# Attention head and token mixer on one core: half-height stores with 8 KB rows, plain relus, narrower pp and another instruction order

## The chip, the cores and the metric

The kernel runs on 1 core of one Trainium2 chip. The metric is device time in microseconds (us). The kernel before takes 110.91 us, the median of 3 runs (110.85 to 111.06).

## What is computed

There are 8 batches of 8 heads, 576 tokens and 64 columns a head. A small set of 32 queries p attends to k and v and packs them; the tokens' queries q then attend to the packed rows. The result, with the heads side by side (576 x 512), goes through a token mixer:

```
p_packed = softmax(p k^T / 8) v
x        = softmax(q p_packed^T / 8) p_packed        # then 576 x 512 per batch
wq, wk   = x w_q, x w_k                              # 512 -> 64 each
W_tok    = (wq wk^T) / 8                             # 576 x 576
out      = relu(W_tok x) w_out                       # 512 -> 512
```

All inputs and the output are float32 in memory; matmuls are made in bfloat16.

## The kernel before

The whole program is one list of steps, ORDER, written out in full and run through from left to right: each item is a step name, a batch and part, an engine (@V is VectorE, DVE; @A ScalarE, ACT; @P GpSimd, POOL) and after "=" the PSUM banks that it takes. PE's steps name no engine. Each engine runs its own steps in the order of the list, and waits for what the others must have done first. DMA issues are steps too: LD steps of q, k, v and w_out (wout) are issued by POOL, because they cast float32 to bfloat16 on the way; K0 and K1 (batch 0's k) and all ST and STF steps (stores) are issued by SyncE (SP); p and w_q, w_k are issued by ACT. An issue stands in its engine's queue like any other instruction.

The steps of a batch b, with their lines:

- LD.k, LD.q, LD.v (L181, L185, L177): 576 KB each at the destination. k and q take one transfer over 128 partitions, v two over 64 partitions each. Four buffers of each kind.
- SET.v (L206): a memset that puts columns of ones at both ends of a v buffer, on DVE.
- KT (L249): 32x32 block transposes of k on DVE. S1 (L261): p times k on PE. X1 (L266): exp on ACT. TE (L270): blocks transposed back on DVE. PV (L282): times v and the ones columns, on PE. RC (L287) and PP (L294): the reciprocal of the row sums, and pp, the packed rows normalised and masked. PT: pp transposed, both on DVE.
- QV: q transposed on DVE in three pieces. S2 (L339): q times the packed rows, on PE. X2 (L344): exp. RS (L354), RR (L359): row sums and reciprocals on DVE. AM (L365): normalised rows, on POOL or DVE, in two or three pieces. AT (L374): transposed on PE. AE: evicted from PSUM.
- QK (L306) and QKE: pp times w_k and w_q. WKQ (L396, L401) and WE: wk and wq. GM (L422), GE, Y (L432), YE: the mixer regrouped so that 576 x 576 is never formed. MX (L446) and MR (L452): W_tok x for 512 and for 64 tokens. RL, RLF, RLR (L457 on ACT, L459 on DVE): relu.
- OT (L491): times w_out, 16 matmuls of 128x512 a batch and 4 for the remaining tokens of two batches. OE, OEF: evicted to SBUF as float32. ST (L511 for the remaining tokens, else L496), STF (L496): stored.

The steps of neighbouring batches are interleaved, so that PE works on the OT of batch b while the attention of b+1 and b+2 runs. WARM steps are matmuls on a zero tile that keep PE busy where it would wait (57 of them). The relu (turn, L464) also puts the tokens into another order on the way, so that in a store each partition holds two neighbouring tokens: a store covers 128 partitions (64 groups times two halves) with 4 KB rows, two of four token tiles at a time. The output has 10 half buffers of 128x1024. A store's place in SP's queue sets when it can go: ST.3.4 is the second in the queue and waits for the remaining tokens of batches 2 and 3.

```
    def turn(eng, o, i):
        relu(eng, o.rearrange("a (t g y) -> a t y g", g=GR, y=2), i.rearrange("a (t y g) -> a t y g", g=GR, y=2))
...
        dst = out[b].rearrange("(g r) n -> g r n", r=R)[:, 0:8].rearrange("g (y t) n -> g y (t n)", y=2)
        nc.sync.dma_start(dst[:, :, t * D:t * D + n], o)
```

Of the kernel before, what the change touches and what calls it, by code (L numbers as in the profile page):

```python
# [7 lines left out]
NL, NB, NO, NE = 4, 3, 10, 2  # L8

ORDER = """  # L10
SET.warm LD.P0 LD.P1 LD.P2 LD.P3 LD.W0 LD.W1 LD.K0 LD.k1 LD.K1 SET.mask@V KC.0@V SET.v0@V LD.v0 PC@V
LD.q0 KT.0.0@V KC.1@A SET.v3@V PX@V KT.0.1@V SET.v1@V WARM.27=0 S1.0=0,1,2,3 SET.idf@V KT.1.2@V
SET.aff@P X1.0.1@A LD.k2 WC.0@P SET.aT0@V TE.0.1@V WARM.4=4 S1.1=4,5,6,7 LD.v1 SET.v2@V X1.1.1@A
X1.0.0@A LD.q1 X1.1.0@A TE.0.0@V LD.v2 SET.aT1@V TE.1.1@V WARM.6=2 PV.0.0=2,3 LD.k4 PV.0.1 QV.0.1@V
WC.1@P QV.0.0@V LD.q2 RC.0.1@V RC.0.0@V PP.0.1@V QV.0.2@V PP.0.0@V PT.0@V LD.k3 KT.2.2@V WARM.9=6
S2.0.2=6,7 S2.0.3=0,1 X2.0.2@A X2.0.3@A SET.idb@V TE.1.0@V RS.0.4@V WARM.5=4 PV.1.0=4,5 LD.O PV.1.1
QK.0=2 RC.1.0@V RC.1.1@V RR.0.4@V S1.2=6,7,0,1 PP.1.0@V AM.0.2@P PP.1.1@V AM.0.3@P PT.1@V WARM.1=3
AT.0.2=3 QV.1.1@V AE.0.2@A QK.1=4 X1.2.0@A SET.aT2@V QV.1.0@V QKE.0@A X1.2.1@A QV.1.2@V WARM.2=5
S2.1.3=6,7 LD.v3 QKE.1@A TE.2.1@V S2.1.2=2,3 AT.0.3=5 X2.1.2@A TE.2.0@V X2.1.3@A AE.0.3@V WARM.1=0
PV.2.0=0,1 RS.1.4@V WKQ.0.0=2,3 WKQ.0.2 WKQ.0.1 PV.2.1 WE.0.2@A RR.1.4@V KT.4.2@V AM.1.2@P WARM.1=4  # L20
GM.0=4 AM.1.3@P GE.0@V RC.2.1@V RC.2.0@V WARM.1=6 Y.0=6 PP.2.1@V S1.4=2,3,4,5 YE.0@V PP.2.0@V
X1.4.1@A MX.0.0=6,7 LD.q3 QV.2.0@V MX.0.1=0,1 RL.0.0@A AT.1.3=4 PT.2@V LD.v4 QV.2.1@V AT.1.2=5
X1.4.0@A AE.1.3@V S2.2.3=6,7 RL.0.1@A LD.q4 QV.2.2@V AE.1.2@V S2.2.2=2,3 KT.3.2@V LD.k5 WKQ.1.0=4,5
X2.2.3@A WKQ.1.1 X2.2.2@A WKQ.1.2 S1.3=0,1,6,7 WE.1.2@A RS.2.4@V QK.2=2 X1.3.1@A GM.1=3 LD.q5
OT.0.2=4,5 X1.3.0@A TE.3.1@V GE.1@A OT.0.0=6,7 RR.2.4@V TE.3.0@V OT.0.3 AM.2.2@V AM.2.3@V OT.0.1
LD.k6 OE.0.1@A TE.4.1@V AT.2.2=3 AT.2.3=0 OE.0.0@A AE.2.2@V Y.1=1 TE.4.0@V PV.3.0=4,5 QKE.2@A YE.1@V
MR.0=6,7 PV.3.1 AE.2.3@V RLR.0@A MR.1=2,3 MX.1.0=6,7 LD.v5 RLR.1@A RC.3.1@V QV.3.1@V WKQ.2.0=0,1
RL.1.0@A MX.1.1=2,3 RC.3.0@V WKQ.2.2 PP.3.1@V WKQ.2.1 PP.3.0@V OT.1.4=6 WE.2.2@A PT.3@V QV.3.2@V
QK.3=7 QV.3.0@V OEF.1.4@A GM.2=4 LD.v6 RL.1.1@V PV.4.0=0,1 ST.1.4 GE.2@A QKE.3@A Y.2=6 PV.4.1 YE.2@V
S2.3.2=4,5 S2.3.3=2,3 RC.4.0@V X2.3.2@A RC.4.1@V PP.4.1@V MX.2.0=6,7 OT.1.2=4,5 PP.4.0@V RL.2.0@A  # L30
QV.4.0@V MX.2.1=0,1 X2.3.3@A QV.4.2@V MR.2=6,7 OT.1.3 PT.4@V QV.4.1@V RLR.2@A RL.2.1@A OT.1.0=2,3
RS.3.4@V OE.1.1@A S2.4.2=6,7 S2.4.3=0,1 OT.1.1 RR.3.4@V X2.4.3@A KT.5.2@V AM.3.3@P OT.2.0=4,5
X2.4.2@A OE.1.0@A RS.4.4@V S1.5=0,1,6,7 OT.2.1 LD.q6 X1.5.0@A AM.3.2@V X1.5.1@A LD.k7 AT.3.3=2
RR.4.4@V QV.5.1@V OE.2.0@A OT.2.2=0,1 AM.4.3@P AE.3.3@V QK.4=3 TE.5.1@V AT.3.2=6 OT.2.3 AE.3.2@A
QKE.4@A KT.6.2@V WKQ.3.0=4,5 AM.4.2@P OE.2.1@A AT.4.3=7 LD.v7 WKQ.3.2 WKQ.3.1 AE.4.3@V AT.4.2=6
S1.6=2,3,0,1 WE.3.2@A AE.4.2@V TE.5.0@V WKQ.4.0=6,7 X1.6.1@A QV.5.0@V GM.3=4 LD.q7 WKQ.4.2 X1.6.0@A
WKQ.4.1 GE.3@V PV.5.0=0,1 TE.6.1@V WE.4.2@A Y.3=5 TE.6.0@V PV.5.1 YE.3@A GM.4=4 RC.5.1@V QV.5.2@V
MX.3.1=2,3 RC.5.0@V GE.4@A MX.3.0=6,7 PP.5.0@V RL.3.1@A PV.6.0=4,5 PP.5.1@V Y.4=0 PT.5@V PV.6.1
RL.3.0@A YE.4@V S2.5.3=2,3 RC.6.1@V RC.6.0@V QK.5=1 PP.6.0@V X2.5.3@A PP.6.1@V OT.3.0=6,7 PT.6@V
QKE.5@A S2.5.2=4,5 QV.6.2@V MX.4.0=2,3 QV.6.1@V MR.3=0,1 X2.5.2@A OT.3.1 RL.4.0@A QV.6.0@V RLR.3@V  # L40
S2.6.2=4,5 RS.5.4@V MX.4.1=2,3 S2.6.3=0,1 X2.6.2@A RL.4.1@A OT.3.4=4 X2.6.3@A RR.5.4@V OT.4.0=2,3
OEF.3.4@V AM.5.3@P OE.3.0@A KT.7.2@V QK.6=5 ST.3.4 ST.1.0 OT.4.1 ST.0.0 ST.1.1 ST.0.1 ST.2.0 ST.3.0
OT.3.2=0,1 RS.6.4@V OE.4.0@A AM.5.2@P AT.5.3=4 QKE.6@A ST.4.0 S1.7=6,7,2,3 ST.2.1 RR.6.4@V AE.5.3@V
AT.5.2=5 AM.6.3@P OT.3.3 X1.7.1@A AE.5.2@A X1.7.0@A WKQ.5.0=2,3 OE.3.1@V OT.4.2=4,5 AM.6.2@P WKQ.5.2
WKQ.5.1 QV.7.2@V ST.3.1 TE.7.0@V AT.6.3=6 WE.5.2@A OT.4.3 AE.6.3@V QV.7.1@V GM.5=7 OE.4.1@A
WKQ.6.0=0,1 GE.5@V AT.6.2=6 TE.7.1@V MR.4=2,3 Y.5=7 WKQ.6.1 AE.6.2@A YE.5@A QV.7.0@V WKQ.6.2 RLR.4@A
PV.7.0=4,5 WE.6.2@A MR.5=6,7 MX.5.0=2,3 PV.7.1 RLR.5@V RL.5.0@A MX.5.1=0,1 GM.6=6 RC.7.1@V RC.7.0@V
PP.7.0@V OT.5.4=7 GE.6@A PP.7.1@V RL.5.1@A PT.7@V Y.6=6 OEF.5.4@V S2.7.0=2,3 YE.6@A S2.7.2=4,5
OT.5.2=0,1 X2.7.2@A ST.5.4 ST.4.1 X2.7.0@A RS.7.2@V S2.7.1=6,7 RS.7.0@V MX.6.1=4,5 MX.6.0=2,3
X2.7.1@A OT.5.3 RR.7.2@V RR.7.0@V RL.6.0@A AM.7.2@P RS.7.1@V OT.5.0=6,7 AM.7.0@V OE.5.1@A RR.7.1@V  # L50
RL.6.1@V QK.7=2 AM.7.1@P AT.7.0=3 ST.5.1 OT.5.1 AE.7.0@A QKE.7@V AT.7.2=0 AT.7.1=1 OE.5.0@A AE.7.2@V
WKQ.7.0=4,5 AE.7.1@V MR.6=2,3 WKQ.7.2 WKQ.7.1 ST.5.0 WE.7.0@V OT.6.0=0,1 WE.7.1@A GM.7=6 OT.6.1
GE.7@A RLR.6@A Y.7=7 OT.6.2=4,5 OE.6.0@V YE.7@A MR.7=2,3 MX.7.1=6,7 ST.6.0 MX.7.0=0,1 RLR.7@V OT.6.3
RLF.7.1.0@A RLF.7.0.1@V RLF.7.1.1@A RLF.7.0.0@V OT.7.4=2 OE.6.1@A OT.7.2=3 OEF.7.4@V ST.6.1 OT.7.3=6
ST.7.4 OEF.7.2@V OT.7.1=7 STF.7.2 OEF.7.3@V OT.7.0=0 STF.7.3 OEF.7.1@V STF.7.1 OEF.7.0@A STF.7.0
# [4 lines left out]
def kernel(  # L60
# [42 lines left out]
    inpool = ctx.enter_context(tc.tile_pool(name="inpool", bufs=NL))  # L103
    bpool = ctx.enter_context(tc.tile_pool(name="bpool", bufs=NB))
    epool = ctx.enter_context(tc.tile_pool(name="epool", bufs=NE))
    opool = ctx.enter_context(tc.tile_pool(name="opool", bufs=NO))
# [44 lines left out]
    p32 = opool.tile([P, L * Dh // 2], fp32, tag="o", name="p32")  # L151
    k32 = [epool.tile([P, RQ * Dh], fp32, tag="e2", name="k32") for _ in range(2)]
    w32 = const.tile([P, 2, 2, 2, Dl], fp32)
    wqk = const.tile([P, 2, 2, 3, Dl], bf16)
    wout = const.tile([P, NJ, D], bf16)
    v_bufs = [const.tile([P, 6, W], bf16, name=f"v_sb{n}") for n in range(NL)]
    k_in, q_in = {}, {}

    def load(x):
        a, b = x[0], x[1:]  # L160
        if a == "K":
            x = int(b)
            nc.sync.dma_start(k32[x], pairs(k, 0)[:, x])
        elif a == "P":
            c = int(b)
            src = p.rearrange("b (i c) (y l) d -> c (b i) y (l d)", i=2, y=2)
            nc.scalar.dma_start(p32[quarter(c)], src[c])
        elif a == "W":
            w = (moe_w_q, moe_w_k)[int(b)].rearrange("(i c j e) m -> (c j) i (e m)", i=2, c=4, e=2)
            nc.scalar.dma_start(w32[:, int(b)].rearrange("a i e m -> a i (e m)"), w)  # L170
        elif a == "O":
            nc.gpsimd.dma_start(wout, moe_w_out.rearrange("(j a) n -> a j n", a=P))
        elif a == "v":
            b = int(b)
            for i in range(2):
                src = v[b, 4 * i:4 * i + 4].rearrange("c (g r) d -> g c (r d)", r=R)
                nc.gpsimd.dma_start(v_bufs[b % NL][halves(i), 1:5], src)  # L177
        elif a == "k":
            b = int(b)
            t = k_in[b] = inpool.tile([P, 2, RQ * Dh], bf16, tag="k_sb", name="k_sb")  # L180
            nc.gpsimd.dma_start(t, pairs(k, b))  # L181
        else:
            b = int(b)
            t = q_in[b] = inpool.tile([P, 2, RQ * Dh], bf16, tag="q_sb", name="q_sb")
            nc.gpsimd.dma_start(t, pairs(q, b))  # L185

    idf = const.tile([P, P], fp32)
    warm = const.tile([P, 512], bf16)
    idb = const.tile([P, P], bf16)
    mask = const.tile([P, 4, Dh], bf16)  # L190
    aT_bufs = [const.tile([P, 2, 640], bf16, name=f"aT{n}") for n in range(NB)]

    def setup(n):
# [11 lines left out]
        elif a == "v":  # L205
            nc.vector.memset(v_bufs[z][:, 0:6:5].bitcast(u32), 0x3F803F80)  # L206
        elif a == "mask":
            zero(mask.rearrange("a x d -> a (x d)"))
            for u in range(4):
                nc.vector.memset(mask[quarter(u), u, :], 1.0)  # L210
# [4 lines left out]
    T = {}  # L215

    def new(key, b, shape, dt=bf16, tag=None, pool=None):
        if (key, b) not in T:
            T[key, b] = (pool or bpool).tile(shape, dt, tag=tag or key, name=key)
# [8 lines left out]
    def KC(x, eng, bk):  # L228
        if 0 not in k_in:
            k_in[0] = inpool.tile([P, 2, RQ * Dh], bf16, tag="k_sb", name="k_sb")  # L230
# [6 lines left out]

    def WC(n, eng, bk):
# [3 lines left out]
        else:  # L242
            copy(eng, wqk[:, :, :, 1], w32[:, 0])
            copy(eng, wqk[:, :, :, 2], w32[:, 0])

    def KT(b, x, eng, bk):
        kT = new("kT", b, [P, 2, RQ, GQ, 2], pool=epool)
        xs = slice(0, 2) if x == 2 else slice(x, x + 1)
        blocks(kT[:, xs].rearrange("a x r g e -> a (x r g e)").bitcast(u32),  # L249
               k_in[b][:, xs].rearrange("a x n -> a (x n)").bitcast(u32))  # L250


    def S1(b, eng, bk):
# [314 lines left out]
```

## Time and profile before

| what | before |
|---|---|
| median of 3 runs | 110.91 us |
| the profiled execution's span, first to last instruction | 110.1 us |
| PE busy, share | 91.8 us, 83% |
| DVE | 87.7 us, 80% |
| ACT | 65.7 us, 60% |
| POOL | 39.0 us, 35% |
| DMA engines' share by POOL's queue (loads) | 71.4% |
| by SP's queue (K and stores) | 25.1% |
| chain that ended last: PE, DVE, ACT, DMA | 42%, 26%, 13%, 7% |

The profile is of one execution and gives its span; the runs' times count what lies around the span too, 0.84 us between this span and the median. In the slices of the span each digit is the busy share of a fortieth (2.75 us) in tenths. The timeline names start, duration, engine, line and operation; in brackets stands how long the engine was idle before and what ended that. A transfer's row gives its size and the time from its issue to its landing. POOL's busy time counts its DMA issues as the profile lists them.

### The profile page before, as it was taken

Reading aid. Unit: us, or ns where it says so; the run is one execution under the profiler, and the core shown is the slowest. Engines: PE = TensorE matmul, PEld = TensorE weight load, DVE = VectorE, ACT = ScalarE, POOL = GpSimd, SP = SyncE. Lnnn points to the kernel's source line nnn. Section 1 sums busy time; section 2 is a strip of 40 time slices with the busy share of each in tenths; the row PEclk is TensorE's granted clock in tenths of the full one; section 3 lists DMA queues with packets and bytes.
Section 4 is the critical chain, followed back from the end, with each engine's and each line's share of the span. In section 5 each row is a group of like instructions: output and inputs, shape, how many; then the busy total and the mean of one; then the engine's idle time right before and its main releaser. Section 6 shows DMA issues by size and latency. Waiting matters only on the chain.

```text
span 110.1 us, 3454 instructions
## 1 busy us (share of the span) xinstructions
PE 91.8 (83%) x1465; PEld 50.8 (46%) x1481; DVE 87.7 (80%) x170; ACT 65.7 (60%) x97; POOL 39.0 (35%) x53
## 2 busy tenths in 40 slices
PE   5992079869486778999999999899999999999940
PEld 2340022445264365565635577644567654654410
DVE  3310995999999997999998999998979779839630
ACT  0062025022473599398699979899874998846220
POOL 3070049940843972424006892000853002300000
PEclk9999656999999999999999999999999999999999
DMA  3999999999999999999999999999999998362594
GB/s 105 334 257 230 214 199 143 185 206 203 214 213 207 210 205 215 204 208 217 209 252 210 204 207 215 210 207 210 242 406 406 394 405 338 134 266 92 213 381 174
DMA packets 13167, 25.71 MB, mean 234 GB/s; under 512 B 992, under 2 KB 6112, under 8 KB 13152
## 3 DMA queue, kind: packets, MB, share of 16 engines
q0 software_dynamic: 8960, 14.09, 71.4%
q1 hardware_dynamic: 3456, 10.62, 25.1%
q10 hardware_dynamic: 736, 0.79, 2.5%
q8 instruction: 11, 0.18, 0.6%
q14 instruction: 4, 0.03, 0.1%
HBM read 30.15 MB, written 9.44 MB: 360 GB/s over the span
## 4 chain that ended last, share of the span: by engine, by line
PE 42%; DVE 26%; ACT 13%; DMA 7%; issue 5%; ACTq 2%; POOL 1%; DVEq 0%; POOLq 0%
PE ps L491 21%; DMA p<-in_p_dram 7%; DVE e L223 6%; ACT relu L457 5%; DVE kT L223 5%; DVE rs L354 4%; ACT e L344 3%; PE ps L339 3%; PE ps L282 3%; PE ps L446 2%; PE ps L374 2%; ACT e1T L266 2%; DVE qT L223 2%; DVE pp L294 2%; DVE aT L135 2%
## 5 line engine op out<-in xcount | busy, mean ns | idle before, releaser
L491 PE MATMUL ps<-wout,relu 128*128 128x512 bf16 x120 | 30.0, 379 | 0.7 <-issue 0.3
L365 POOL TENSOR_TENSOR a<-e,rr 128x256 bf16<-128x256 f32 (+2 forms) x13 | 16.0, 1244 | 35.1 <-DVE rr L359 14.9
L457 ACT ACTIVATE relu<-ps 128x1024 bf16<-128x1024 f32 (+1 forms) x14 | 17.1, 1242 | 1.8 <-PE ps L446 1.4
L535 PE MATMUL ps<-warm 128*128 128x512 bf16 x52 | 16.0, 449 | 1.6 <-DVE warm L138 1.2
L491 PEld LDWEIGHTS <-relu 128*128 128x128 bf16 x128 | 11.4, 98 | 12.1 <-issue 1.4
L131 ACT ACTIVATE o<-ps 128x1024 f32<-128x1024 f32 (+1 forms) x13 | 12.8, 996 | 6.5 <-PE ps L491 6.5
L266 ACT ACTIVATE e1T<-ps 128x576 bf16<-128x576 f32 x16 | 9.9, 661 | 11.0 <-PE ps L261 8.7
L344 ACT ACTIVATE e<-ps 128x256 f32<-128x256 f32 (+2 forms) x17 | 11.0, 675 | 6.1 <-PE ps L339 5.9
L354 DVE TENSOR_REDUCE rs<-e 128x40 f32<-128x1280 f32 (+2 forms) x10 | 12.1, 1209 | 1.6 <-ACT e L344 1.5
L177 POOL DMA_DIRECT2D v_sb<-in_v_dram x16 | 10.1, 634 | 8.8 <-DVE v_sb L206 4.0
L223 DVE STREAM_TRANSPOSE e<-e1T 128x576 bf16<-128x576 bf16 x16 | 11.9, 756 | 1.3 <-ACT e1T L266 1.2
L223 DVE STREAM_TRANSPOSE qT<-q_sb 128x512 uint32<-128x512 uint32 (+1 forms) x24 | 12.7, 549 | 0.0
L223 DVE STREAM_TRANSPOSE kT<-k_sb 128x1152 uint32<-128x1152 uint32 (+1 forms) x9 | 10.9, 1207 | 0.0
L535 PEld LDWEIGHTS <-warm 128*128 128x128 bf16 x57 | 5.8, 110 | 9.6 <-issue 4.9
L261 PE MATMUL ps<-kT,pT 32*32 32x288 bf16 x256 | 5.0, 328 | 5.2 <-DVE pT L223 4.8
L339 PE MATMUL ps<-ppT,qT 64*128 64x64 bf16 x320 | 7.3, 190 | 2.1 <-DVE ppT L223 1.1
L282 PE MATMUL ps<-v_sb,e 64*64 64x192 bf16 x288 | 8.6, 247 | 0.5 <-DVE e L223 0.4
L131 ACT ACTIVATE wkq<-ps 128x896 bf16<-128x896 f32 (+1 forms) x8 | 7.0, 878 | 3.0 <-PE ps L401 3.0
L339 PEld LDWEIGHTS <-qT 64*128 64x128 bf16 x320 | 6.1, 94 | 5.7 <-issue 2.5
L374 PE MATMUL ps<-idb,a 128*128 128x128 bf16 x80 | 6.8, 220 | 1.0 <-POOL a L365 1.0
L282 PEld LDWEIGHTS <-e 64*64 64x64 bf16 x288 | 6.0, 106 | 2.9 <-DVE e L223 1.8
L294 DVE SCALAR_TENSOR_TENSOR pp<-ps,rec,mask 128x256 bf16<-128x256 f32 x16 | 7.1, 478 | 0.3
(58 smaller groups left out, 126.4 us busy)
## 6 DMA issues: line engine op xcount, KB each, us to landing
out_dram<-o SPq DMA_DIRECT2D x14, 512.0 KB, 4.5
v_sb<-in_v_dram POOLq DMA_DIRECT2D x16, 288.0 KB, 11.7
q_sb<-in_q_dram POOLq DMA_DIRECT2D x8, 576.0 KB, 12.3
k_sb<-in_k_dram POOLq DMA_DIRECT2D x7, 576.0 KB, 13.7
k<-in_k_dram SPq DMA_DIRECT2D x2, 576.0 KB, 5.1
out_dram<-o_rem SPq DMA_DIRECT2D x4, 256.0 KB, 3.6
out_dram<-o SPq DMA_DIRECT2D x4, 256.0 KB, 2.7
p<-in_p_dram ACTq DMA_DIRECT2D x4, 128.0 KB, 7.9
```

What stands on the lines that cost most here:

```text
L131: nc.scalar.activation(o, i, COPY)
L177: nc.gpsimd.dma_start(v_bufs[b % NL][halves(i), 1:5], src)
L223: nc.vector.transpose(o, i)
L266: nc.scalar.activation(e1T[:, cc], T["s1", b][cc], EXP, scale=scale)
L282: nc.tensor.matmul(T["pv", b][halves(cc), i, cc * Dh:(cc + 3) * Dh], lhsT, rhs, start=n == 0, stop=n == R - 1, skip_group_check=True)
L339: nc.tensor.matmul(ps[:, y, t - t0, i], lhsT, rhs, start=e == 0, stop=e == 1)
L344: nc.scalar.activation(e2[:, t0:t1].rearrange("a t (i y n) -> a y (t i) n", i=2, y=2), T["s2", b, c].rearrange("a y t i n -> a y (t i) n") ...
L354: nc.vector.tensor_reduce(rs[:, t0 * H:t1 * H], e2v(b, c), axis=AX, op=ADD)
L365: e.tensor_tensor(a2[:, t0:t1].rearrange("a t i (u l) -> a (t i u) l", l=L), e2v(b, c), T["rr", b][:, t0 * H:t1 * H].to_broadcast((P, (t1 ...
L457: nc.scalar.activation(o, i, RELU)
L491: nc.tensor.matmul(ps, lhsT, wout[:, j, :], start=j == 0, stop=j == NJ - 1)
L535: nc.tensor.matmul(ps, warm[:, 0:P], warm, start=True, stop=True)
```

## The change

Several things change together. The steps and their arithmetic stay the same.

- The order of all steps is another one, with 84 warm matmuls instead of 57. Of the start, k's two halves of batch 0, one quarter of p and w_q are issued by SP, w_k and three quarters of p by ACT. p is converted on ACT (PC@A), and both halves of k on DVE.
- The memsets of the ones columns (SET.v) are POOL's, and those of v0 and v2 stand behind the loads into the same buffers.
- pp keeps two heads side by side instead of four: its tile and its mask are half as wide, PT half as long, and QK takes 8 matmuls over 64 rows instead of 4 over 128. The third copy of w_q in wqk is dropped; a step QD copies it in pqk instead (POOL seven times, DVE once).
- relu reorders tokens for batch 7 alone (TURN). For batches 0 to 6 it is a plain copy; k is transposed into another layout (KT), which puts four neighbouring tokens on one partition. Such a batch is stored by two transfers of 64 partitions with rows of 8 KB each. Output buffers hold a whole batch (128x4x512), 6 of them, and the float32 copies of p, w and the identity share their space.
- The last store (STF.7.0) is issued by ACT.
- Tiles are allocated one by one instead of from rotating pools. DIAG is empty, so the branches for it do nothing.

The diff, cut to its core (of ORDER the stretch that holds the first batches' loads, and the stores):

```diff
-NL, NB, NO, NE = 4, 3, 10, 2
+NL, NB, NO, NE = 4, 3, 6, 2
+DIAG = ()
+TURN = (7,)
...
-SET.warm LD.P0 LD.P1 LD.P2 LD.P3 LD.W0 LD.W1 LD.K0 LD.k1 LD.K1 SET.mask@V KC.0@V SET.v0@V LD.v0 PC@V
-LD.q0 KT.0.0@V KC.1@A SET.v3@V PX@V KT.0.1@V SET.v1@V WARM.27=0 S1.0=0,1,2,3 SET.idf@V KT.1.2@V
...
+SET.warm@V LD.K0@S LD.K1@S LD.W1@A LD.P3@S LD.P1@A LD.P0@A LD.P2@A SET.idf@V LD.k1 LD.v0 LD.q0
+KC.0@V KC.1@V KT.0.1@V LD.W0@S PC@A PX@V KT.0.0@V SET.aT0@V SET.aff@P SET.idb@V KT.1.2@V WARM.30=4
+S1.0=0,1,2,3 X1.0.1@A X1.0.0@A TE.0.1@V SET.v0@P SET.v1@P WARM.4=6 S1.1=2,3,4,5 X1.1.0@A WC.0@A
+LD.v1 TE.0.0@V WARM.5=0 PV.0.0=2,3 LD.q1 SET.mask@P LD.k2 X1.1.1@A PV.0.1 RC.0.0@V RC.0.1@V SET.v3@P
+PP.0.0@V PP.0.1@V PT.0@V WC.1@P QV.0.2@V QV.0.0@V QV.0.1@V WARM.13=0 QK.0=2 S2.0.2=0,1 TE.1.0@V
+X2.0.2@A S2.0.3=4,5 X2.0.3@A TE.1.1@V QKE.0@V RS.0.4@V LD.v2 SET.v2@P LD.q2 WARM.4=3 PV.1.0=0,1
+PV.1.1 RC.1.0@V RR.0.4@V SET.aT1@V RC.1.1@V QD.0@V PP.1.1@V QV.1.0@V PP.1.0@V PT.1@V QV.1.2@V
+QV.1.1@V AM.0.2@V LD.k3 AM.0.3@P LD.O WARM.15=4 QK.1=0 QKE.1@A QD.1@P AT.0.3=4 AE.0.3@V S2.1.3=2,3
...
+PV.6.0=2,3 QKE.5@V PV.6.1 RC.6.1@V RC.6.0@V QD.5@P LD.q7 AT.5.2=4 OE.3.1@A AE.5.3@A AE.5.2@A ST.1.0
+ST.0.1 ST.1.4 ST.2.0 ST.3.4 ST.0.0 ST.3.0 ST.2.1 MX.4.1=0,1 MX.4.0=6,7 RL.4.1@A WKQ.5.0=4,5 PP.6.0@V
...
+RLF.7.0.0@A RLF.7.1.0@A RLF.7.1.1@V OT.7.4=3 OT.7.3=6 ST.3.1 ST.5.4 ST.1.1 ST.4.1 ST.4.0 ST.5.0
+ST.5.1 ST.6.0 ST.6.1 OEF.7.4@A OEF.7.3@A OT.7.2=5 OT.7.1=6 OT.7.0=3 OEF.7.2@A ST.7.4 STF.7.3
...
         elif a == "v":
-            nc.vector.memset(v_bufs[z][:, 0:6:5].bitcast(u32), 0x3F803F80)
+            eng.memset(v_bufs[z][:, 0:6:5].bitcast(u32), 0x3F803F80)
...
-        kT = new("kT", b, [P, 2, RQ, GQ, 2], pool=epool)
+        kT = new("kT", b, [P, 2, R, 2 * GQ, 2], bufs=NE)
...
-        pp = new("pp", b, [P, 2, 2, 2 * Dh])
+        pp = new("pp", b, [P, 2, 2, Dh])
...
+    def QD(b, eng, bk):
+        w = T["pqk", b]
+        copy(eng, w[:, :, 2 * Dl:], w[:, :, Dl:2 * Dl])
...
-    def turn(eng, o, i):
-        relu(eng, o.rearrange("a (t g y) -> a t y g", g=GR, y=2), i.rearrange("a (t y g) -> a t y g", g=GR, y=2))
+    def turn(b, eng, o, i):
+        if b in TURN:
+            o = o.rearrange("a (t g y) -> a t y g", g=GR, y=2)
+            i = i.rearrange("a (t y g) -> a t y g", g=GR, y=2)
+        relu(eng, o, i)
...
+    def ST(b, n, eng, bk):
+        q = nc.scalar if eng == "A" else nc.sync
+        if n == 4:
             dst = out.rearrange("b (g r) n -> (b g) r n", r=R)
+            q.dma_start(dst[(b - 1) * GR:(b + 1) * GR, R - 1], T["orem", b // 2])
+        elif b in TURN:
...
+        else:
+            q.dma_start(orows(b)[:, n], T["o", b][halves(n)].rearrange("a t n -> a (t n)"))
```

## The prediction

> **What bounds the kernel now.** I read, in this order, the slices of the span, the busy times by stretches of ten microseconds, the chain that ended last, POOL's timeline, and the transfers. First two of the slices:
>
> ```profile
> DVE  3310995999999997999998999998979779839630
> DMA  3999999999999999999999999999999998362594
> ```
>
> ```profile
> 20.00:30.00 10.00, 7.54 (x168) 4.33 (x163) 9.79 (x23) 2.51 (x6) 5.45 (x8) 1.00 1.16 201
> 40.00:50.00 10.00, 9.58 (x163) 5.80 (x165) 9.31 (x17) 7.89 (x13) 3.27 (x6) 1.00 1.18 209
> 80.00:90.00 10.00, 9.86 (x190) 6.35 (x191) 8.55 (x18) 7.91 (x14) 2.49 (x2) 1.00 1.02 403
> ```
>
> (The columns of the stretches are busy time of PE, PE's weight load, DVE, ACT and POOL, then granted clock, DMA share and GB/s.) DVE is full from 11 to 80 us, PE from 43 us to the end, and the DMA engines carry a load without a gap until 80 us. Now the chain:
>
> ```profile
> 42.72 0.45 PE ps L422 x10
> 43.18 0.22 PE ps L491
> ...
> 100.52 5.30 PE ps L491 x24
> 105.84 0.60 ACT o L131
> ```
>
> ```profile
> wout<-in_moe_w_out_dram POOLq DMA_DIRECT2D x1, 512.0 KB, 19.2
> ```
>
> ```profile
> 23.70 0.77 POOL L172 DMA_DIRECT2D wout<-in_moe_w_out_dram  x1 [1.11 <-DMA v_sb<-in_v_dram]
> 27.91 2.48 POOL L365 TENSOR_TENSOR a<-e,rr 128x256 bf16<-128x256 f32 x2 [3.44 <-DVE rr L359]
> ```
>
> wout is issued at 23.70 and lands 19.2 later, at 42.9; the first output matmul (L491, step OT.0.2) starts at 43.0. From there PE does not stop: I gave each step in PE's order its warm time from the timeline (an OT step 4 matmuls in 0.86, S1 0.49, both PV steps 0.99, S2 0.85, a batch's WKQ 0.85, AT 0.56, QK 0.33, GM 0.29, Y 0.23, an MX 0.22, MR 0.17). That is 72.6 us for the program, 13.0 of it before OT.0.2 and 59.6 after; PE takes 62.8 for those 59.6. So the end is the start of OT.0.2, plus the PE work behind it at 1.05, plus a tail of 4.3 (105.8 to 110.1: last eviction, last store). What starts OT.0.2 is what matters.
>
> **What the change moves onto that path: POOL.** Before, the four memsets of the ones columns (L206) are DVE's, ahead of their loads. After, they are POOL's, and those of v0 and v2 stand *behind* the loads into the same buffers. The changed instruction order shows the memset of v2 waiting on the two semaphores of the v2 load; behind it on POOL stand, in order, the issues of q2 and k3, AM.0.3 (1024 columns, now POOL's first product), and the issue of wout. POOL is in order, so AM.0.3 can't start before v2 has landed.
>
> When does v2 land? Seven load units of 576 KB come first in both kernels (k1, v0, q0, k2, v1, q1, v2; the changed order puts k2 last but one), behind the same K, P and W. Before, the second half of v2 was issued at 19.5 and took 11.9:
>
> ```profile
> v_sb<-in_v_dram POOLq DMA_DIRECT2D x1, 288.0 KB, 11.9
> ```
>
> 31.4 us. After, v1 is issued behind the memsets of v0 (v0 landed at 15.2 before: issued 6.8, 8.4 on the way) and v1: at 15.2 + 2 x 0.75 = 16.7 instead of k2's 15.5. A POOL memset of this size isn't in the trace: DVE's took 538 ns, POOL's cast of 128x256 0.38 to 0.45 us, which would be 0.95 for 576 columns; I take 0.75, the middle. k2's first packets came 2.4 us after its issue, and the load queue's share fell to 80 and 77% in 16 to 18 us. So v2 lands 0.6 later, at 32.0. Then memset 0.75, two issues of 0.73: AM.0.3 runs from 34.1 to 36.0 (1.907, row L365). Before, it ended at 30.4. DVE's rr, which released it then (27.75), may be late by up to 6 us without being felt, which covers the start: P behind W1 on ACT's queue, and the conversion of P on ACT behind its table load (1.28 + 1.04 instead of 0.69 on DVE).
>
> From 36.0 on, by rows: AT.0.3 0.6, AE.0.3 0.67 and AE.0.2 0.2 (DVE, 37.6), KT.2.2 1.34 (39.0), meanwhile S2.1, X2.1 1.4 (38.7), WE.0.2 0.93 (39.6), GM 0.35, GE 0.3 behind an X1 of 0.66, Y, YE, MX.0 (42.2). On DVE RS.1.4 1.47 and RR 0.4 (40.9), two TE and two QV (43.5), both RC, QV.2.2, two PP, PT (45.1), AE.1.3 0.67, KT.3.2 1.34 (47.0). PE's order puts S1.3 (needs KT.3.2) and WKQ.1.1 ahead of OT.0.2: it starts at 48.0, not 43.0. wout, issued behind AM.0.3 in a queue that still holds k3, lands near 43.2 and no longer decides.
>
> Price on the path: +5.0 at OT.0.2, with 12.4 instead of 13.0 us of PE work done, so +5.6.
>
> **What it removes.** DVE: 16 PP of half width (478 ns; 345 is my estimate, from 0.16 fixed and 1.04 ns a column as the two widths of kT show; between 290 and 478) -2.1; 8 PT (435 to 288, the row of qT 128x128) -1.2; memsets of v -2.2; evictions that went to ACT or came from it -2.7 in sum. 8.2 of 95.7 us of summed DVE durations. Behind KT.3.2 58 us remain, where 62 did. PE needs 60 there, so DVE's relief no longer sets the end; I count none of it, and as much as 3 us if PE's stalls (62.8 for 59.6) were all DVE's. ACT: ten plain relus cost between 1029 ns (the plain eviction of the same size) and 1326: at most -3.0, but ACT takes five OEF (+3.0), AE (+2.5) and PC; -1.1 net, hidden beside PE. POOL +5.0, seven QD copies among it; the others wait behind work that comes anyway. QK: 8 matmuls of 128 columns on half rows for 4 of 192; L446's half-row pairs run side by side, so 0 to -0.1 each, taken as nothing. The 27 added warm matmuls stand where PE waits.
>
> **The stores.** Rows of 8 KB: no packet here is above 4608 bytes; 4096 cost 163.5 ns, 2048 cost 86.8, so a packet has some 10 ns of its own, and even if 8 KB went as one, all stores together would save 0.3 us of 16 engines. Nothing. When they go matters more: SP is in order, and before it held back behind ST.3.4 until 77.7.
>
> ```profile
> q1 hardware_dynamic: 144, 0.26, 8.1%
> ...
> out_dram<-o_rem SPq DMA_DIRECT2D x1, 256.0 KB, 7.9
> ```
>
> That one early store, at 52, took 7.9 instead of 3.2, and by the packets the load queue fell from 1.1 to 0.75 of the engines beside it: stores take 30%. After, ST.1.0, ST.0.1, ST.1.4 and ST.2.0 (1.8 MB) go as soon as OE.1.1 is done, near 65. Loads: q2 finds the queue empty, starts at 32.7 + 2.4 = 35.1, and at 2.81 us a unit (31.4 to 79.5 for 16 units, wout and that store) q5 lands at 62.9; seven units at 70% from 66.5 end at 89.4 (q7; before 79.5). S2.7 would come at 48.0 + 45.0 x 1.05 = 95.2: 4 us to spare, so it costs nothing, but only because the rest is late.
>
> **The sum.** S2.7 at 95.2; behind it 15.2 us of PE work at 1.035 (16.05 for 15.5 before): 110.9; tail 4.3: span 115.2. The median of the runs, 110.91, is 0.84 above the profiled span of 110.07: **116.0**.
>
> **Rivals.**
> (a) *64 partitions are slow to read.* The nearest rows are the v loads, 64 partitions each: packets of 1152 bytes in 107 ns where 2304 of the 128-partition loads take 196, 9% more a byte. If a store takes twice the time, 6.7 MB are left at 89.4, 5.1 of them in half-height stores: 25.3 + 3.9 us at 202 and 403 GB/s, end at 118.6, with the last landing 1.5 later and 0.84: about 120.9. For: such a store reads half of the partitions only. Against: P, 32 partitions high, shows its packets at 159 ns. [...]
> (b) *Only the stores hurt.* If the chain from AM.0.3 is absorbed (OT.0.2 by 44), stores start at 61.5, q7 lands at 91.6, S2.7 follows at 93.3, PE ends at 109: 114.1.
> (c) *Faster: DVE is the bound.* If rr and v2 come so that AM.0.3 starts by 29, OT.0.2 starts at wout's 43.2, PE's stalls shrink to 2% and early stores leave the loads alone: 43.2 + 61.4 + 4.3 + 0.8 = 109.7. For it: DVE full until 80. It decides if AM.0.3 starts before 29 and q7 lands before 86.
> (d) *Nothing is seen:* the lateness and DVE's relief cancel, 110.9.
>
> One more row: PE stood idle from 9.1 to 13.9 and its granted clock was 0.62 in 11 to 20. After, PE idles some 6 us before AT.0.3. At half clock the 2.5 us of PE on the way to OT.0.2 would cost 1 more, inside the range. [...]
>
> **Chances.** Forecast 0.50, (a) 0.20, (b) 0.15, (c) 0.12, (d) 0.03. A measurement of this kernel tells 0.2% from no change. Slower: 0.85; same 0.03; faster 0.12. The range takes in (b), the memset's and the relief's bounds below (112.5) and most of (a) above (120.5).
>
> **What would show it.** In the changed profile: POOL's AM.0.3 at 34, its memset released by the v2 transfer; no load packets between about 32 and 35; OT.0.2 near 48; q7 landing near 89; S2.7 near 95. It is wrong if AM.0.3 starts by 30, if OT.0.2 starts by 44, or if DMA and not PE ends the chain.

## The result, and the profile after

The changed kernel takes 129.74 us (median of 4 runs, 129.23 to 130.07), the kernel before 110.98 beside it: a ratio of 1.168, with an interval of 1.164 to 1.172. It is slower, as forecast, but by 18.8 us and not by 5, and outside the range. Some executions of a kernel are two to four per cent longer than its others; times below are medians of all executions, ratios leave the long ones out, so the two can differ by a per cent.

The slices of the changed kernel's span (PE, DVE, granted clock, DMA share and GB/s; 3.2 us each):

```profile
PE   6980599990189999999699999799930599998910
DVE  1241939891068988599999998999602926986000
PEclk9999779998559999999999999999995559999997
DMA  4999979992899999999999999999871059749992
GB/s 142 348 248 209 210 109 201 204 206 35 121 211 198 188 160 213 208 212 210 208 212 237 314 239 295 206 316 331 147 207 31 5 163 204 204 87 255 282 332 114
```

Two holes go through PE, DVE, clock and DMA alike: one at 29 to 35 us, one at 93 to 101. By stretches (columns as in the prediction):

```profile
20.00:30.00 10.00, 8.61 (x120) 4.35 (x120) 8.76 (x23) 1.79 (x3) 0.36 (x1) 1.00 1.06 191
30.00:40.00 10.00, 4.70 (x99) 3.52 (x102) 3.19 (x4) 2.37 (x4) 6.07 (x8) 0.66 0.80 136
40.00:50.00 10.00, 9.68 (x180) 5.53 (x181) 9.49 (x18) 7.49 (x13) 7.31 (x9) 1.00 1.10 187
90.00:100.00 10.00, 4.20 (x81) 2.70 (x81) 3.38 (x7) 5.51 (x9) 2.48 (x2) 0.80 0.56 120
```

The first hole is the one that was forecast. POOL's timeline, and wout's transfer:

```profile
30.82 0.58 POOL L204 MEMSET v_sb<- 128x576 uint32 x1 [10.45 <-DMA v_sb<-in_v_dram]
31.34 0.71 POOL L183 DMA_DIRECT2D q_sb<-in_q_dram  x1
...
32.77 1.93 POOL L396 TENSOR_TENSOR a<-e,rr 128x1024 bf16<-128x1024 f32 x1
34.63 0.81 POOL L172 DMA_DIRECT2D wout<-in_moe_w_out_dram  x1
```

```profile
wout<-in_moe_w_out_dram POOLq DMA_DIRECT2D x1, 512.0 KB, 7.7
```

wout lands at 42.3, some 6 us before it is used. The second hole is in the later part of the chain that ended last:

```profile
34.76 1.04 PE ps L405 x8
...
48.10 0.22 PE ps L432 x2
48.32 0.21 PE ps L526
...
84.56 0.29 POOL pqk L133
84.85 0.17 issue
85.01 13.51 DMA q_sb<-in_q_dram
98.54 1.31 DVE qT L231 x2
...
100.08 0.44 DVE pqk L135
...
100.56 0.59 PE ps L526
...
105.63 1.01 PE ps L370 x40
...
120.94 1.47 PE ps L526 x6
122.43 0.60 ACT o L131
```

L526 is the output matmul now (OT), L405 AT, L370 S2, L133 at 84.56 QD.5. POOL issues q7's load only at 85.01, behind QD.5. The load takes 13.5 us. Who waited, in 92 to 102 us:

```profile
DVE qT L231 <- DMA q_sb<-in_q_dram: 6.5, 1, 6.5
PE ps L526 <- DVE pqk L135: 6.3, 1, 6.3
```

DVE waits in QV.7.0 for q7; behind it on DVE stands QKE.6, which frees PSUM bank 6, and PE's next step, OT.5.4, takes that bank. And the stores' transfers, the page of the kernel before first, then that of the changed one:

```profile
out_dram<-o SPq DMA_DIRECT2D x14, 512.0 KB, 4.5
out_dram<-o SPq DMA_DIRECT2D x14, 512.0 KB, 6.7
```

### The profile page after: what moved, and what is told of

Its sections match the earlier page's. It is cut to its first block, busy times and chain, and to the rows that moved or that the text cites. A ratio compares the mean times of both kernels' runs of the same rounds, so it can differ in the third digit from the quotient of the medians.

```text
span 128.3 us, 3577 instructions
## 1 busy us (share of the span) xinstructions
PE 98.9 (77%) x1519; PEld 54.1 (42%) x1540; DVE 82.6 (64%) x163; ACT 66.0 (51%) x102; POOL 44.2 (34%) x62
## 4 chain that ended last, share of the span: by engine, by line
PE 35%; DMA 28%; DVE 15%; POOL 8%; ACT 6%; issue 4%; POOLq 0%; ACTq 0%; DVEq 0%
DMA v_sb<-in_v_dram 17%; PE ps L526 16%; DMA q_sb<-in_q_dram 11%; DVE qT L231 3%; PE ps L405 3%; PE ps L370 3%; DVE a L396 3%; PE ps L432 2%; PE ps L309 2%; DVE rs L385 2%; ACT relu L489 2%; PE ps L427 2%; POOL v_sb L204 2%; POOL v_sb L177 2%; POOL a L396 2%
## 5 line engine op out<-in xcount | busy, mean ns | idle before, releaser
L526 PE MATMUL ps<-wout,relu 128*128 128x512 bf16 x117 | 30.9, 388 | 0.9 <-issue 0.2
L396 POOL TENSOR_TENSOR a<-e,rr 128x1024 bf16<-128x1024 f32 (+2 forms) x13 | 17.7, 1378 | 23.5 <-DVE rr L390 10.4
L572 PE MATMUL ps<-warm 128*128 128x512 bf16 x77 | 21.1, 415 | 2.1 <-DVE warm L138 1.2
L131 ACT ACTIVATE o<-ps 128x1024 f32<-128x1024 f32 (+1 forms) x16 | 14.7, 918 | 6.7 <-PE ps L526 6.5
L526 PEld LDWEIGHTS <-relu 128*128 128x128 bf16 x128 | 11.6, 99 | 12.4 <-issue 1.4
L572 PEld LDWEIGHTS <-warm 128*128 128x128 bf16 x84 | 8.1, 105 | 11.8 <-issue 4.0
L405 PE MATMUL ps<-idb,a 128*128 128x128 bf16 x80 | 7.4, 231 | 7.0 <-POOL a L396 5.9
L489 ACT ACTIVATE relu<-ps 128x1024 bf16<-128x1024 f32 (+1 forms) x12 | 11.6, 975 | 1.2 <-PE ps L478 0.9
L133 POOL COPY pqk<-pqk 128x128 bf16<-128x128 bf16 x7 | 2.0, 290 | 21.5 <-ACT pqk L131 8.0
L526 PE MATMUL ps<-wout,rem 128*128 128x512 bf16 x13 | 4.3, 435 | 6.6 <-DVE pqk L135 6.3
L204 POOL MEMSET v_sb<- 128x576 uint32 x4 | 2.3, 590 | 20.2 <-DMA v_sb<-in_v_dram 20.2
L405 PEld LDWEIGHTS <-a 128*128 128x128 bf16 x80 | 5.1, 102 | 9.8 <-POOL a L396 6.9
L135 DVE COPY aT<-ps 128x1024 bf16<-128x1024 bf16 (+2 forms) x10 | 4.2, 435 | 7.3 <-PE ps L405 7.2
```

The source lines that it names most:

```text
L131: nc.scalar.activation(o, i, COPY)
L396: e.tensor_tensor(a2[:, t0:t1].rearrange("a t i (u l) -> a (t i u) l", l=L), e2v(b, c), T["rr", b][:, t0 * H:t1 * H].to_broadcast((P, (t1 ...
L405: nc.tensor.transpose(ps[:, i, t - t0], T["a2", b][:, t, i], idb)
L489: nc.scalar.activation(o, i, RELU)
L526: nc.tensor.matmul(ps, lhsT, wout[:, j, :], start=j == 0, stop=j == NJ - 1)
L572: nc.tensor.matmul(ps, warm[:, 0:P], warm, start=True, stop=True)
```

## The experiments

Two theories stood at first. *Order*: POOL asks for v2's followers and for q7 too late, and the stores' form is harmless. *Shape*: stores of 64 partitions with 8 KB packets are slow or crowd out the loads. Ratios are to the kernel before, run beside each, with their 95% intervals. The kernel before took 110.7 to 111.0 throughout.

**e1, e2, e3: the two steps on POOL, singly and together.**

```diff
-... QD.5@P LD.q7 AT.5.2=4 ...        # e1, e3
-LD.v7 AM.5.3@P
+LD.v7 LD.q7 AM.5.3@P
-LD.v2 SET.v2@P                       # e2, e3
+SET.v2@P LD.v2
```

> The changed kernel with one step moved: POOL issues q7's load right behind v7's, ahead of AM.5.3 and QD.5. First theory (order on POOL, the load was asked for too late): q7 is issued at about 76 instead of 85.0, lands 90 to 91 behind v7, PE's idle time at 94 to 100 goes, S2.7 starts at 97 to 98 instead of 105.6, and the time is 129.7 - 8 - 1 (clock) = 120.5, within 1.5. Second theory (stores of 64 partitions with 8 KB packets hold the loads up whenever they meet): q7 still lands at 95 or later and the time is 126 or more. Third theory (the amount of early stores, not their shape): like the first here, with q7 at 92 to 93 and 122.

> The changed kernel with one pair of steps exchanged: the memset of v2's edge columns stands ahead of v2's load on POOL. First theory: POOL no longer waits 10.4 us, q2 and k3 are issued by 21.5, the load queue stays full, wout lands at 38 to 39 and OT.0.2 starts at 43 to 44 instead of 48.3; what follows is 4 to 5 us earlier, q7's late load included (it hangs on QKE.5), so the time is 125, within 1.5. If q7's load and the stores set the end by themselves, the time stays above 128.5.

> Both moves, v2's memset ahead of its load and q7's load behind v7's. First theory: the two losses add up, 129.7 - 9 - 5 = 115.7, within 2; PE has no idle stretch over 2 us behind OT.0.2. Second theory (shape of the stores): 121 or more, q7 later than 90.

e2 came as the order theory said: 123.6 us (1.114 [1.108, 1.120]), q2 and k3 issued at 21.1 and 21.8, wout at 39.1, first OT at 42.5. e1 did not: 125.3 (four runs, from 122.4 to 127.5). q7 was asked for 8.5 us sooner and landed only 3.7 sooner, 18.3 us after its issue:

```profile
76.48 18.29 DMA q_sb<-in_q_dram
```

v7, ahead of it in the queue, landed at 87.7; q7's packets ran from about 85 to 94.1, 9 us for 576 KB that take 2.8 where loads are alone. The third theory, by which q7 lands at 92 to 93, isn't met by this profile either. e3 gave 119.5 (117.5 to 121.4), q7 at 90.0, between the first two theories. So these two steps are worth some 10 us of the loss (10.3 by the medians, 11.7 by the shortest runs), and something else holds q7 back.

**e4: plain relu and 64-partition stores alone, on the kernel before.**

```diff
+TURN = (7,)                                   # relu plain for batches 0 to 6
-        store(b, 2 * tp, T["o", (b, tp)]...)
+        nc.sync.dma_start(halves8(b)[:, n], T["o", b][halves(n)]...)   # 64 x 8 KB
```

> The kernel before with only the plain relu copies and the 8 KB stores of 64 partitions for batches 0 to 6 (6 us of relu and layout; order of all steps kept, stores moved behind the second half of their batch; five output buffers of four tiles in place of ten of two). Its loads are done at 79.6 and its stores begin there. First theory: the two parts that name the change cost nothing by themselves, 110 to 112. Second theory (the shape costs): 113 to 117, with stores that land half as fast as before's.

115.7 (1.041 [1.033, 1.050]): the shape theory. Here the stores begin when the loads are done, and still they are slow. The stretch from 78 to 90 us, first before, then e4:

```profile
78.00:90.00 12.00, 11.86 (x202) 7.40 (x203) 10.55 (x19) 9.40 (x15) 3.86 (x4) 1.00 0.99 382
```

```profile
78.00:90.00 12.00, 11.97 (x219) 7.08 (x198) 10.05 (x22) 9.20 (x18) 2.75 (x3) 1.00 1.00 270
```

The engines are as full (DMA share 0.99 and 1.00), and move 270 GB/s where before moved 382. e4's last matmul ends at 103.3, but its span at 113.8: a tail of 10.5 us in place of 4.3, all of it stores.

**e5, e6: the changed kernel with all batches turned (128 partitions, 4 KB packets)**, without and with the two moves on POOL.

```diff
-TURN = (7,)
+TURN = (0, 1, 2, 3, 4, 5, 6, 7)
```

> The changed kernel with TURN set to all eight batches: relu copies turn the positions again and every store takes 128 partitions with 4 KB rows; order of all steps as in the changed kernel. First theory (order on POOL alone): q7 is still asked for at 85 and the time stays within 1.5 of 129.7. Second theory, now wider (64 partitions are read slowly, and where a load's 2304-byte packet waits for an 8192-byte store packet on each DMA engine it gets 2304/(2304+8192) = 0.22 of the bytes, against 0.36 beside 4096): early loads come 1 to 2 us sooner, q7 lands at 93 to 95 instead of 98.5, the store behind it is not late, 123 to 126.

> Both moves on POOL (v2's memset ahead of its load, q7's load behind v7's; 119.5 with the 64-partition stores) and in addition all batches turned and stored by 128 partitions with 4 KB rows. First theory: 119 to 121, the shape is no part of it and the turned relu costs up to 1. Second theory: q7 lands at 87 to 88 instead of 90.0 and PE's wait of 2.5 for it goes, with the tail 1 shorter: 115 to 116.5.

124.2 (1.111 [1.103, 1.119]) and 115.8 (1.041 [1.034, 1.049]), both as the second theory said: the form of the stores is worth 5.6 and 3.7 us in this order (the second is less sure, because e3's runs spread over four us; by the shortest runs it is 2.6). Through q7 it is worth less than expected: q7's last packet ends at 95.5 in e5, where the changed kernel has 98.3, and at 88.6 in e6, where e3 has 89.4 (landed at 89.2, not at 87 to 88). The tail from the last matmul to the end is 4.2 us in both, 5.9 in the changed kernel and in e3. The idea behind these expectations can be counted in the traces' packets, in stretches where both queues had work (KB of 1024 bytes):

| run, stretch (us) | load packets | store packets | loads, KB/us |
|---|---|---|---|
| changed, 69.5 to 72.5 | 107 of 2304 B | 92 of 8192 B | 80 |
| changed, 77.5 to 78.5 | 33, nearly all 1152 B | 38 of 8192 B | 38 |
| e6, 66 to 67 | 48 of 2304 B | 48, 44 of them 4096 B | 108 |
| e6, 67.2 to 68.8 | 91 of 2304 B | 89, 79 of them 2048 B | 128 |

About one packet for one in these stretches, whatever their sizes; loads alone moved some 200 KB/us (193 in 35 to 60 of the changed kernel, 204 in 45 to 51 of the kernel before). So beside 8 KB packets a load had about a quarter of the bytes in the first of them, and a v load, with 1152 bytes, a ninth in the second. It isn't so in every stretch: e6 has 9 load packets to 91 of stores in 85 to 86, when most of q7 had come, and the trace doesn't tell on which engine a packet ran.

**e7, e8: one store of 128 partitions a batch with the plain relu.**

```diff
-q.dma_start(orows(b)[:, n], T["o", b][halves(n)]...)      # twice
+q.dma_start(orows(b).rearrange("g y n -> y g n"), T["o", b]...)   # once, outermost dimension 2
```

> Both moves on POOL and the plain relu, but each batch 0 to 6 is stored by one transfer of 128 partitions with 8 KB rows instead of two of 64. If the 64 partitions are what is slow: these stores land at full rate, about 390 KB a microsecond where nothing loads, and their packets take 322 ns, not 640; where they meet loads the packets are as long as before and q7 lands no sooner than 89: 116 to 118. If packets of 8 KB are slow whatever the partitions: 119 to 121.

> The kernel before with the plain relu, and one store of 128 partitions with 8 KB rows for each of batches 0 to 6 (the run with two of 64 took 115.7, its store queue busy from 76 to 112 at some 250 KB a microsecond). If the 64 partitions are slow: stores at some 390 KB a microsecond as before's, 109.5 to 111.5. If the 8 KB packets are slow: 114 to 116.

Both theories missed: 224.4 and 222.3, twice the time. e8 in 79 to 118:

```profile
79.00:118.00 39.00, 21.26 (x256) 12.15 (x258) 13.97 (x29) 14.86 (x26) 4.09 (x4) 0.83 0.13 55
```

6.5 packets a us of 310 ns each keep 2.0 of the 16 engines busy, as many as the transfer's outermost dimension has entries. These two runs say nothing of packets or partitions.

**e9: 8 KB packets from 128 partitions, on the kernel before.** With the turned layout a partition's 8 KB are one row of the output:

```diff
-store(b, 2 * n, T["o", b][:, 2 * n:2 * n + 2]...)      # twice, 128 x 4 KB
+store(b, 0, T["o", b]...)                              # once, 128 x 8 KB
```

> The kernel before with its turned relu kept and each of batches 0 to 6 stored by one transfer of 128 partitions with 8 KB rows (a row is one partition's whole 8 KB here, so the outermost dimension has 128 entries); five output buffers of four tiles. It differs from the run with two stores of 64 partitions (115.7) in the partitions and the relu, not in the size of the packets. If 64 partitions are slow: packets of 8192 bytes take about 320 ns, stores move 380 to 400 KB a microsecond, 110 to 112. If packets of 8 KB are slow: many take 640 ns, 114 to 116.

112.3 (1.012 [1.008, 1.016]), a little over the range of the first theory, and of the 896 packets of 8192 bytes all but 3 are under 500 ns, 318 in the mean. With 64 partitions they took 495 in e4 (54% over 500) and 443 in the changed kernel (38%). So it is the partitions, not the packets. The 1.2% that stay, for stores that have to wait for a whole batch, were not taken apart.

**e10, e12: stores held back until the loads are over**, both with the moves on POOL, e10 turned, e12 as changed.

```diff
-ST.1.0 ST.0.1 ST.1.4 ST.2.0 ST.3.4 ST.0.0
+ST.3.4 ST.1.0 ST.0.1 ST.1.4 ST.2.0 ST.0.0
```

> Both moves on POOL and all batches stored by 128 partitions (115.8), and ST.3.4, which waits for an eviction at 78 or later, put ahead of the four early stores, so that no store meets the loads before then. If the alternation of load and store packets on the DMA engines is what keeps q7 late: v7 lands at 79 to 80 and q7 at 82 to 84 in place of 89.2, PE doesn't wait for it, 112 to 114. If q7 is no longer what the end hangs on: 115 to 117.

> Both moves on POOL, the plain relu and stores of 64 partitions as in the changed kernel (119.5), and ST.3.4 ahead of the four early stores, so that stores begin at 79 or later. The alternation theory: q7 lands at 82 to 84 instead of 90.0, PE doesn't wait, but all stores are still to go then at 250 to 300 KB a microsecond, so that their queue is busy to the end: 114 to 118. If early stores were no harm: 119 to 121.

q7 landed at 80.3 and 80.7, PE did not wait for it, and yet: 115.9 (1.043 [1.036, 1.049]), no better than e6, and 118.6 (1.067 [1.060, 1.073]), between its two ranges. In this order the end doesn't hang on q7 once it comes by 89 (e6). In e12 the last matmul ends at 107.7 and the span at 116.5: the tail is 8.8, 4.1 in e10.

**e11: the changed code under the order of before**, all batches turned, QD.b behind each QKE.b.

> The code of the changed kernel (pp over head pairs, copies by QD, six output buffers) under the order of the kernel before, with QD.b on POOL right behind each QKE.b, and all eight batches turned and stored by 128 partitions. If the loss lies in order and stores alone: DVE's relief of some 8 us is worth 0 to 2 where PE sets the pace, 108.5 to 111. If the narrow head itself costs (more and smaller matmuls, QD on the way to WKQ): 112 to 115.

111.2, a ratio of 1.000 [0.996, 1.005]. The narrow head costs nothing and brings nothing that this interval shows, though DVE's summed durations fall from 95.7 to 92.5 us. Between e10 and e11 the order differs, with the engines that it names: 4.7 us. Both profiles start OT.0.2 at 43.4 or 43.5; the last matmul ends at 109.9 and 106.6. PE's waits behind 43 us sum to 3.3 in e10 and 0.9 in e11; e10's largest:

```profile
PE ps L405 <- DVE a L396: 1.1, 1, 1.1
PE ps L309 <- DVE e L231: 1.0, 1, 1.0
PE ps L484 <- DVE y L472: 0.4, 1, 0.4
```

These are AM.3.2 (DVE), a TE and a YE, each late once. With the 0.6 us more of PE work that this order leaves behind OT.0.2 (an estimate, from the warm times of the prediction), that is 3.0 of the 3.3 us between the last matmuls. But e11's profiled execution took 112.9, 1.7 above its median, so the profiles show 2.9 of the 4.7 us (spans of 114.0 and 111.1); the rest isn't seen.

**e13, e16: the upper halves' stores on POOL's queue**, so that both halves are read together; e13 on e4, e16 on e12.

```diff
-... ST.1.1 ST.0.1 ST.2.1 ...
+... ST.1.1@P ST.0.1@P ST.2.1@P ...
```

> The kernel before with plain relu and two stores of 64 partitions for each of batches 0 to 6 (115.7, tail from the last matmul to the end 10.5), with the stores of partitions 64 to 127 issued on POOL's queue and those of 0 to 63 on SP's, so that both halves are in flight together. If one half of the partitions is read at a reduced rate: few packets of 8192 bytes over 500 ns, stores at 350 to 400 KB a microsecond, the tail back at 4 to 6, and since the plain relu lets the last matmul end 2.5 earlier (103.3 against 105.8), 108.5 to 111. If something else makes them slow: 113 to 116.

> The changed kernel's order with both moves on POOL and the early stores held back (118.6, last matmul at 107.6, tail 8.9), and the upper halves' stores on POOL's queue. If one half at a time is the cause: the tail falls to 4 to 5.5, 114 to 115.5. If not: 117.5 to 119.

115.0 (1.032 [1.027, 1.038]), where "something else" had been put, and 120.4 (1.084 [1.079, 1.089]), above both ranges. e13's stretches show why: while both queues had stores, and when all or nearly all of them were on one:

```profile
81.00:89.00 8.00, 7.97 (x149) 5.19 (x147) 6.64 (x16) 6.64 (x12) 1.86 (x4) 1.00 1.00 364
89.00:93.00 4.00, 3.54 (x36) 1.62 (x35) 3.79 (x8) 2.86 (x4) 1.66 (x2) 1.00 1.00 250
102.00:105.00 3.00, 2.68 (x13) 1.00 (x11) 2.07 (x3) 0.28 (x1) 0.32 (x1) 1.00 0.88 175
```

A packet of 8192 bytes took 360 ns in the first stretch (181 packets from POOL's queue, 172 from SP's), 524 in the second and 656 in the third, with the same packets throughout. With e9, whose single queue read 128 partitions at 318 ns a packet, that leaves one half of the partitions at a time as what is slow. But at the end stores come one by one; that this is what cost e13 its time is tested by e17. In e16 SP's queue alone had store packets of 8 KB at 80 to 84 and 91 to 97, POOL's alone at 98 to 101 and 106 to 108; e16 tells nothing either way.

**e14: the transposes of q7 moved behind OEF.5.4 on DVE**, q7's load left late.

```diff
-AE.6.2@V QV.7.0@V QV.7.1@V RC.7.1@V QKE.6@V ... PP.7.0@V QV.7.2@V PP.7.1@V ... OEF.5.4@V
+AE.6.2@V RC.7.1@V QKE.6@V ... PP.7.0@V PP.7.1@V ... OEF.5.4@V QV.7.0@V QV.7.1@V QV.7.2@V
```

> The changed kernel with the three transposes of q7 (QV.7.0, QV.7.1, QV.7.2) moved on DVE behind OEF.5.4, so that QKE.6 no longer stands behind the wait for q7; q7's load is as late as before the move (98.5). If q7 was needed at QKE.6 and so at OT.5.4: OT.5.4, WKQ.6 and OT.5.2 run at 93 to 97 while q7 is awaited, S2.7 starts at 100 to 101 instead of 105.6, and the time is 125, within 1.5. If S2.7 is where q7 is needed: no change, 129 to 130.5.

125.5 (1.127 [1.119, 1.134]), q7 at 98.8, and on PE:

```profile
95.03 1.04 PE L526 MATMUL ps<-wout,rem 128*128 128x512 bf16 x4
...
96.69 1.03 PE L526 MATMUL ps<-wout,relu 128*128 128x512 bf16 x4
100.41 0.77 PE L370 MATMUL ps<-ppT,qT 64*128 64x64 bf16 x40 [2.69 <-DVE qT L231]
```

OT.5.4 no longer waits, and S2.7 starts at 100.4 instead of 105.6. q7 was needed at QKE.6.

**e15, e17, e18: putting it together.** e15 is e11 with the plain relu and halves on two queues; e17 (on e13) and e18 (on e15) keep the plain form for batches 0 to 3, whose stores stand close together at 77 to 92, and turn the rest.

```diff
-TURN = (7,)
+TURN = (4, 5, 6, 7)                  # e17, e18
```

> The order of the kernel before with the narrow head, the plain relu, stores of 64 partitions for batches 0 to 6, and the upper halves on POOL's queue. If one half of the partitions at a time is the cause and the order was the rest: 111.2 (turned, order of before) less some 2 for the plain relu, 108 to 110. If the stores are still slow: 113 to 116.

> The kernel before with plain relu and two stores of 64 partitions, on two queues, for batches 0 to 3 alone; batches 4 to 7 turned and stored by 128 partitions. If the loss of the run with seven plain batches (115.0) was the stores of one half at a time behind 89: the tail from the last matmul is 4 to 5 again, 109.5 to 111.5. If not: 113 or more.

> The order of the kernel before with the narrow head and the same mixture, plain halves on two queues for batches 0 to 3, turned stores of 128 partitions for 4 to 7. If the loss of 113.7 with seven plain batches was the stores of one half at a time: 109 to 111. If not: 112.5 or more.

e15 113.7 (1.022 [1.017, 1.027]), in the range of "still slow", as e13 was; e17 111.0 (1.000 [0.997, 1.004]) and e18 110.4 (0.9945 [0.991, 0.998]), both as the theory of one half at a time said. Taking the half-height stores from the end gives back what they cost. e18 is the shortest of all, half a per cent under the kernel before: a small gain, but its interval ends below 1; its last matmul ends at 104.1 and its span at 108.9, a tail of 4.8.

## Why the prediction was right and wrong

What separates the two kernels, step by step of the runs: the narrow head 0.3, which is not told from nothing (e11), the order with both moves on POOL 4.7 (e10), early stores of 128 partitions -0.1 (e6), plain relu and 64-partition stores 3.7 (e3), and the two steps on POOL 10.3 (changed against e3). Unrounded that is 18.8. The last two share e3, whose runs spread over four us, so each is known to some two us only, and the steps don't add up the same way in another sequence (the form alone was worth 2.7 to 5.6).

- *What bounds the kernel*: start of OT.0.2, PE behind it, tail. Right for before, and for e11.
- *The memset of v2*: right as a mechanism. v2 landed at 30.7 (32.0 forecast), POOL's memset took 0.58 (0.75), AM.0.3 ran from 32.8 to 34.7 (34.1 to 36.0), KT.3.2 ended at 46.9 (47.0), OT.0.2 came at 48.2 (48.0). That the last one fits to 0.2 is in part luck: AM.0.3 was 1.3 early, and the stretch behind it 1.5 longer than forecast. PE had been idle for 5.9 us and ran at a granted clock of 0.50 until 38, so that AT.0.3 took 1.04 and not 0.6; the prediction named this at 1 us and left it out of its sum. e2 takes the wait away alone and gains 6.2 us.
- *DVE's relief, counted as none*: right as far as it was tested. Its summed durations fell by 5.4 us (95.7 to 90.3) and not by 8.2; e11 has 3.2 of that alone, and gains nothing.
- *The plain relu, counted as nothing*: mis-sized a little. From OT.0.2 to the last matmul's end e4 takes 61.8 us where before takes 62.8, e12 65.5 where e10 takes 66.5: 1.0. (That e4's OT.0.2 also starts 1.5 earlier is not the relu's: wout was issued at 22.4 there and at 23.7 before, ahead of any relu.)
- *8 KB rows, "Nothing"*: right of the packets (e9), wrong of the transfers, which are read from 64 partitions. Rival (a) named that mechanism and priced it at 120.9; alone it costs 4.8 (e4 against before; 3.5 against e9, which also stores whole batches), 2.7 where the stores come late (e12 against e10), 3.7 beside the loads (e3 against e6). Its price had every such store at half rate, which was the author's assumption: e4 moved 270 GB/s in 78 to 90 us where before moved 382, single stretches of e13 175 to 250, and e13's first stretch, with both halves in flight by two queues, 364; the early ones, beside loads, had packets of 322 ns in 69 to 72 us. P's packets, held against the rival with 159 ns, took 172 for the most part (87 of 128; 20 took 159) and ran beside other transfers too.
- **The step that failed is that of the early stores: "seven units at 70% from 66.5 end at 89.4", and S2.7 at 95.2, "4 us to spare, so it costs nothing".** Three things in it were wrong.
  - First, q7 was taken to follow v7 in the queue, but POOL issued it at 85.01, behind QD.5, which waits for QKE.5. The prediction followed what stands behind v2's memset on POOL, and not what stands ahead of q7's issue; of the work that POOL takes on, QD copies among it, it said that "the others wait behind work that comes anyway".
  - Second, the loads were taken to keep 70% of their rate beside stores, from a store with 2 KB packets; beside 8 KB packets they kept 80 of some 200 KB/us while it lasted (69.5 to 72.5). Up to v7 this was worth one or two us, because the early stores did not fill the time: v7's last packet ended at 86.8, and the forecast's rate gives 85.4. But in e1, where only the issue is moved, q7 landed 7 us behind v7, at 94.8, and not 4.0.
  - Third, the need was put at S2.7; it was at QV.7.0, ahead of QKE.6 on the in-order DVE, and so at OT.5.4 (e14).

  q7 landed at 98.5. Stores are not all of its 13.5 us: the load queue ran empty at 86.8, its first packet came at 89.2, and in 90 to 94 its packets took 273 ns in the mean where 192 is usual, with only 31 store packets of 8 KB beside 163 of its own. S2.7 came at 105.6: 10.4 late, 6.3 of it PE's wait, some 2.4 (an estimate, half of PE's 4.78 busy us) that PE then lost at half clock, as the stretch behind the wait shows, and 1.7 that was not taken apart:

```profile
101.00:106.00 5.00, 4.78 (x41) 2.54 (x42) 2.34 (x5) 0.92 (x2) 0.00 (x0) 0.50 0.39 108
```

- *Behind S2.7*: 16.8 instead of 15.7 to the last matmul, tail 5.9 instead of 4.3, and 1.4 instead of 0.84 between the span and the median; with the 10.4 this makes the 13.7 us between 116.0 and 129.7. In the tail half-height stores again stand ahead of batch 7's: 8 KB packets until 123, at 425 to 502 ns from 118 on (means of 2 us). The 0.84 is not what lies around the span: in the runs on record time and span differ by 1.8 or so (129.23 and 127.3, 110.82 and 109.0), so the profiled execution of the kernel before was about 1 us longer than the median.
- Rivals (b) and (c) needed OT.0.2 by 44; it came at 48.2. (d) is out by the result.

What stays open: e9's 1.2%; which of the order's single waits weighs how much in the 4.7 us, and 1.8 of them that no profile shows; what the 1.7 us of S2.7's lateness are, and why q7's packets were slow in 90 to 94; and why, in e4, 27% of the 8 KB packets take about 309 ns, 38% take 600 or more and the rest lie between.

## What to carry to other kernels

For the last load of each kind, look at who stands ahead of its issue on the issuing engine, and who stands behind its first reader on the reader's engine: the need is where the reader blocks its queue, not where the data is used (e14: 125.5 us against 129.7). Store from 128 partitions (packets of 8192 bytes took 318 ns in e9, 495 from 64 partitions in e4), and not with an outermost dimension of 2 (e8: 222.3 us). Where stores ran beside loads, the loads kept 80 of some 200 KB/us beside packets of 8192 bytes, 108 and 128 where most had 4096 and 2048. That counts only where a load is awaited: holding the stores back brought q7 in 9 us sooner in e10 and gained nothing.

## What the hardware showed that was not expected

- In four stretches where loads and stores both had work, about one packet of the one went for one of the other, whatever the sizes: 107 to 92 and 33 to 38 (changed kernel), 48 to 48 and 91 to 89 (e6). In 85 to 86 of e6 it was 9 to 91.
- Transfers with an outermost dimension of 2 kept 2.0 of 16 engines busy, at 55 GB/s (e8).
- Packets of 8192 bytes read from 64 partitions took 495 ns in the mean (e4), from 128 partitions 318 (e9), from both halves by two queues 360 (e13, 81 to 89 us).
- q7's load, issued at 85.0, showed its first packet only 4.2 us later: v7's ran until 86.8, and from 87 to 89 the engines moved stores alone. q2's first packet, with the engines free, had come 1.4 us after its issue (31.3 to 32.75).
